# An attention and token-mixing block on one core: weight conversions queued in program order with the channel mixer's activations, and weight loads in larger groups

## The chip, the cores and the metric

The kernel runs on one core of a Trainium2 chip. A core has a matrix engine (TensorE, PE in the profile), a vector engine (VectorE, DVE), an engine for activations (ScalarE, ACT), a general engine (GpSimd, POOL) and SyncE (SP), whose queue issues the DMA transfers here. Each engine works through its own queue in order. Matrix products land in PSUM banks, from which DVE and ACT take them to SBUF. The metric is the device time of one execution in microseconds (us); lower is better.

## What is computed

The reference, cut to what matters (batch 8, 8 heads, 576 rows, head width 64, 128 features; model width 512, hidden width 2048):

```python
def phi(x):
    proj = np.einsum('bhsd,df->bhsf', x, w_phi)
    proj = proj - np.max(np.abs(proj), axis=-1, keepdims=True)
    return np.concatenate([np.exp(proj), np.exp(-proj)], axis=-1)
q_p, k_p = (phi(q), phi(k))
kv = np.einsum('bhsf,bhsd->bhfd', k_p, v)
num = np.einsum('bhsf,bhfd->bhsd', q_p, kv)
den = np.einsum('bhsf,bhf->bhs', q_p, np.sum(k_p, axis=2))[..., None] + 1e-06
x = (num / den)                      # then heads side by side: [8, 576, 512]
u = x + (x.transpose(0, 2, 1) @ U @ V).transpose(0, 2, 1)
out = u + np.maximum(u @ w_ch1, 0.0) @ w_ch2
```

U, V, w_ch1 and w_ch2 come as float64. [...]

## The kernel before

**Stages.** A `Pair` is the attention of two heads of one batch entry; there are 32 pairs. `Tokens` is the U and V product of one batch entry, which starts when its four pairs are done. `Mixer` g is the channel mixer (u @ w_ch1, relu, @ w_ch2) of the 512 rows that batch entry g gives; a ninth mixer takes the remaining 64 rows of all eight. The work of Mixer g is put between the steps of the attention of batch entry g + 1.

**The mixer.** The hidden width goes in 16 tiles of 128. For tile f, `hidden(f)` makes 12 products of 512 columns into one PSUM bank `ph` (L565); ACT takes the relu of it as `h_hi` (L570), DVE the remainder as `h_lo` (L571); `add(f)` makes 12 products into four banks `o` (L582). Each float32 operand is split into a high and a low part, hence the pairs of tiles `uT_hi`/`uT_lo`, `h_hi`/`h_lo`, `w1`/`w2` with two parts. There is one bank `ph` for all mixers but the last, so `hidden(f + 1)` starts only when `h_lo` of tile f has been made. The order in which PE meets these is: ph of tile f, what is left of o of tile f - 1 with attention work between, o of tile f with `h_hi`, ph of tile f + 1, o of tile f with `h_lo`.

**The weights.** The two weight matrices have 16 tiles each, so there are 32 blocks; block `w1_f` is needed by `hidden(f)` and block `w2_f` by `add(f)`, and all mixers use the converted blocks. `load_weights` (L201, L204) issues the loads of one pair of blocks (`words`) on the SP queue; the table `LOADS` says up to which tile they are issued at each of the first pairs. `convert` makes a float32 block from the words: three activations on ACT (L137, L138, L140), two operations on DVE (L141, L142) and one 64-bit addition on GpSimd (L146). `split_w` then splits it: a copy (L223; on ACT for w1, on DVE for w2) and a subtraction on DVE (L224). So a block costs ACT three or four instructions, DVE three or four, GpSimd one. Their work tiles `w_ab` take four buffers, which they share with the split `xs` of the tokens (L507, L508).

**What sets the order.** The program text says when a block is converted: `Pace.step`, called once in each attention step, converts blocks at an even rate between step 24 and step 63, and `mix` converts a block at the latest when the first mixer needs it. The text's order does not bind the engines' queues, though. A scheduler takes the instructions with their dependencies and orders each engine's queue by its own estimate of when each can start. It may put a conversion ahead of an activation that the text has earlier. `tc.issue_after(ins)` takes that freedom away for a block of code: every instruction in it that goes to the engine of `ins` stands behind `ins` in that queue. It adds no wait on a semaphore.

**Names in the rows.** `pp`, `pst`, `vp` are the tokens' products, `pt` the transposes of u, `kv_ps`, `pq`, `pk`, `xp`, `T` those of the attention; `qp`, `kp` are the features, `mk` a maximum, `den` the denominator. In an instruction order, `w2_3_ab` is the work tile of block w2_3, `h_lo0_6` is `h_lo` of Mixer 0 and tile 6; a number behind the name is that of the buffer.

Of the kernel before, what the change touches and what calls it, by code (L numbers as in the profile page):

```python
# [16 lines left out]
AF = mybir.ActivationFunctionType  # L17
# [8 lines left out]
def tile_kernel(  # L26
# [12 lines left out]
    nc = tc.nc  # L39
# [30 lines left out]
    def ps(name, tag="at"):  # L70
        return psum.tile([P, 512], F32, tag=tag, bufs=BANKS[tag], name=name)

    def f32(ap):
        return ap.bitcast(F32)
# [55 lines left out]
    def convert(st, name):  # L130

        n = st.shape[1]
        halves = st.rearrange("p n w -> p (n w)").bitcast(U16).rearrange("p (n h) -> p n h", h=4)
        ab = scratch(f"{name}_ab", I32)
        a, b_ = ab[:, 0, 0:n], ab[:, 1, 0:n]
        bh = b_.bitcast(U16).rearrange("p (n h) -> p n h", h=2)
        nc.scalar.activation(out=bh[:, :, 0], in_=halves[:, :, 1], func=AF.Copy, scale=2.0 ** -13)  # L137
        nc.scalar.activation(  # L138
            out=bh.bitcast(F16)[:, :, 1], in_=f32(st[:, :, 1]), func=AF.Copy, scale=2.0 ** -60)
        nc.scalar.activation(out=f32(a), in_=f32(st[:, :, 1]), func=AF.Abs, scale=2.0 ** -48)  # L140
        nc.vector.tensor_scalar_max(out=f32(a), in0=f32(a), scalar1=2.0 ** -63)  # L141
        nc.vector.tensor_scalar(  # L142
            out=a, in0=a, scalar1=3, scalar2=None, op0=ALU.logical_shift_left)

        a64, b64 = a.bitcast(U64), b_.bitcast(U64)
        nc.gpsimd.int64_add(a64, a64, b64)  # L146
        return f32(a)
# [41 lines left out]
    LAST = NFC - 1  # L189

    def place(f, dt, shape, name):

        if f == LAST:
            both = home.tile([P, 2, *shape], dt, tag="w_last", name=name)
            return both[:, 0], both[:, 1]
        return [home.tile([P, *shape], dt, tag=f"w{n}_{f}", name=f"{name}_{n}") for n in (1, 2)]
# [9 lines left out]
    def convert_block(i):  # L206
        f, n = divmod(i, 2)
        r = convert(words[f][n], f"w{n + 1}_{f}")
        if f < LAST:
            w = home.tile([P, 2, C], F32R, tag=f"w{n + 1}_{f}", name=f"w{n + 1}_{f}")  # L210
            split_w((nc.scalar.copy, nc.vector.tensor_copy)[n], r, w)
        elif n == 0:
            found[f] = r
            return
        else:
            w1_w, w = place(f, F32R, (2, C), f"w_{f}")
            split_w(nc.scalar.copy, found[f], w1_w)
            split_w(nc.vector.tensor_copy, r, w)
            w1_t[f] = w1_w
        (w1_t, w2_t)[n][f] = w  # L220

    def split_w(copy, r, w):
        copy(out=w[:, 0, :], in_=r)  # L223
        nc.vector.tensor_sub(w[:, 1, :], r, f32(w[:, 0, :]))  # L224

    def w1_part(f, part, c):
        return w1_t[f][:, part, c * P:(c + 1) * P]
# [314 lines left out]
    class Mixer:  # L542
# [17 lines left out]
        def hidden(self, f):  # L560
            ph = ps(f"ph{self.g}_{f}", "at" if self.g >= B - 1 and f % 2 == 0 else "ph")
            n = 0
            for c in range(NCC):
                for l, r in ((0, self.uT_hi), (0, self.uT_lo), (1, self.uT_hi)):
                    nc.tensor.matmul(  # L565
                        ph, w1_part(f, l, c), r[:, c, :], start=(n == 0), stop=(n == 3 * NCC - 1))
                    n += 1
            h_hi = moe.tile([P, 512], F32R, tag="h_hi", bufs=2, name=f"h_hi{self.g}_{f}")
            h_lo = moe.tile([P, 512], F32R, tag="h_lo", bufs=2, name=f"h_lo{self.g}_{f}")
            nc.scalar.activation(out=h_hi, in_=ph, func=AF.Relu)  # L570
            nc.vector.scalar_tensor_tensor(  # L571
                out=h_lo, in0=ph, scalar=0.0, in1=f32(h_hi), op0=ALU.max, op1=ALU.subtract)
            self.h[f] = (h_hi, h_lo)

        def add(self, f):
            if self.o is None:
                self.o = [ps(f"o{self.g}_{t}", "o") for t in range(4)]
            h_hi, h_lo = self.h.pop(f)
            for t in range(4):
                cs = slice(t * P, (t + 1) * P)  # L580
                for n, (l, r) in enumerate(((h_hi, 0), (h_hi, 1), (h_lo, 0))):
                    nc.tensor.matmul(  # L582
                        self.o[t], l[:, cs], w2_t[f][:, r, :],
                        start=(f == 0 and n == 0), stop=(f == NFC - 1 and n == 2))
            if f == NFC - 3 and self.g < B:
                self.res = []
                for t in range(0, 4, 2):
                    st = scratch(f"st{self.g}_{t}")
                    nc.sync.dma_start(out=st, in_=u_dram[self.g][:, t:t + 2, :])
                    self.res += [st[:, 0, :], st[:, 1, :]]  # L590
            if f == NFC - 1:
                self.finish()
# [28 lines left out]
    loaded, converted = [0], [0]  # L621

    def weights(upto):

        while loaded[0] <= min(upto, LAST):
            load_weights(loaded[0])
            loaded[0] += 1

    def blocks(upto):
        while converted[0] < min(upto, 2 * NFC):  # L630
            convert_block(converted[0])
            converted[0] += 1

    todo = []
# [1 line left out]
    def mix(n=1):  # L636
        for _ in range(n):
            if todo:
                fn, f = todo.pop(0)
                if fn.__self__.g == 0:  # L640
                    blocks(2 * f + (2 if f == LAST or fn.__name__ == "add" else 1))
                fn(f)
# [3 lines left out]
    class Pace:  # L646
# [5 lines left out]
        def step(self):  # L652

            steps[0] += 1
            blocks((steps[0] - CONVERT[0]) * 2 * NFC // (CONVERT[1] - CONVERT[0]))
            if pieces:
                pieces.pop(0)()
                if not pieces:
                    self.chunks, self.steps = 32 - HELD, BATCH - steps[0]
                else:  # L660
                    keep_busy(1, True)
                return
            n = (self.at + 1) * self.chunks // self.steps - self.at * self.chunks // self.steps
            self.at += 1
            mix(n)
            if not self.chunks:

                keep_busy(1, True)
# [10 lines left out]
            if here:  # L679
                tc.keep_in_program_order(ins)  # L680

    LOADS = (-1, 1, 3, 6, 9, 12, LAST)
    CONVERT = (24, 63)
    BATCH = 67
    pieces = []
# [62 lines left out]
    if True:  # L748
# [17 lines left out]
        for n, (b, j) in enumerate(pairs):  # L766

            far = Pair(*pairs[n + 2]) if n + 2 < len(pairs) else None
            if n < len(LOADS):

                with tc.issue_after(far.loaded.ins):
                    weights(LOADS[n])
            if far is not None:
# [78 lines left out]
```

## Time and profile before

| | us |
|---|---|
| median of 3 runs | 1281.81 |
| the runs | 1281.37, 1281.81, 1289.95 |
| the profiled execution | 1279.61 |
| its span in the trace, from first to last instruction | 1277.8 |

The profiled execution is 1.8 us longer than its span and 2.2 us under the median.

The profile's rows are read so. A stretch of the span is given with the busy time of each engine in it and, in brackets, its instructions. `PEclk` is the share of TensorE's full clock that was granted. An instruction in order of time has its start, its duration, its engine and line, what it writes and reads, and in square brackets for how long the engine sat idle before it and what ended that. A wait is given as engine, instruction, line, then what it waited for, then total us, times, longest.

### The profile page before, as it was taken

The numbers are of one execution on the slowest core, as the hardware profiler recorded it, in microseconds if no ns is written. First come the engines' busy times: TensorE is split into PE (matmuls) and PEld (weight loads), VectorE is DVE, ScalarE is ACT, GpSimd is POOL, SyncE is SP. The second block draws the span as 40 slices with busy tenths as digits, with TensorE's granted clock in tenths as the row PEclk, the third lists the DMA queues.
The fourth block names the chain that finished last, engine by engine and source line by source line (L and its number), as shares of the span: only waits on it lengthen the run. The fifth ranks groups of instructions, "written<-read, shape, count | busy, mean of one in ns | idle before, by whom it ended". The sixth has DMA issues, their size and how long they took to land.

```text
span 1277.8 us, 17927 instructions
## 1 busy us (share of the span) xinstructions
PE 1240.0 (97%) x6939; PEld 1062.0 (83%) x6941; DVE 649.2 (51%) x1441; ACT 540.3 (42%) x1151; POOL 201.2 (16%) x154
## 2 busy tenths in 40 slices
PE   8988979999999999999999999999999999999997
PEld 7766868878888888888888888888888888788886
DVE  5879585565456545455556545545545542211211
ACT  6887484444443444344444435344434431111110
POOL 3444242101110111111110111011111110000000
PEclk9998989999999999999999999999999999999999
DMA  5582131220122111211112012211122002100001
GB/s 137 172 275 72 62 125 28 61 85 25 38 60 80 29 29 45 82 62 29 45 45 89 13 28 68 90 28 29 45 78 66 17 1 87 66 1 1 33 1 33
DMA packets 90100, 75.38 MB, mean 59 GB/s; under 512 B 51488, under 2 KB 76448, under 8 KB 89888
## 3 DMA queue, kind: packets, MB, share of 16 engines
q1 hardware_dynamic: 90016, 74.24, 19.1%
q8 instruction: 55, 0.90, 0.3%
q14 instruction: 29, 0.24, 0.1%
HBM read 55.35 MB, written 18.87 MB: 58 GB/s over the span
## 4 chain that ended last, share of the span: by engine, by line
PE 88%; DVE 6%; ACT 3%; issue 1%; DMA 1%; SPq 0%; POOL 0%; DVEq 0%; POOLq 0%; ACTq 0%
PE ph L565 31%; PE o L582 30%; PE kv_ps L411 7%; PE xp L450 7%; PE T L291 2%; PE pk L371 2%; PE pp L521 1%; PE pq L394 1%; PE kv_ps L404 1%; PE xpt L437 1%; DVE w L224 1%; PE pq L395 1%; PE pt L553 1%; DVE w_ab L141 1%; DVE w_ab L142 1%
## 5 line engine op out<-in xcount | busy, mean ns | idle before, releaser
L565 PE MATMUL ph<-uT_hi,w 128*128 128x512 f32 x1152 | 388.8, 396 | 7.5 <-DVE h_lo L571 6.6
L582 PE MATMUL o<-w,h_hi 128*128 128x512 f32 x1152 | 326.1, 395 | 1.0 <-ACT h_hi L570 1.0
L565 PEld LDWEIGHTS ph<-uT_hi,w 128*128 128x128 f32 x1152 | 217.3, 189 | 51.7 <-DVE h_lo L571 7.8
L582 PEld LDWEIGHTS o<-w,h_hi 128*128 128x128 f32 x1152 | 211.5, 188 | 43.0 <-ACT h_hi L570 2.4
L571 DVE SCALAR_TENSOR_TENSOR h_lo<-ph,h_hi 128x512 fp32r<-128x512 f32 x144 | 99.4, 690 | 265.9 <-ACT h_hi L570 265.2
L565 PE MATMUL ph<-uT_lo,w 128*128 128x512 f32 x576 | 228.4, 396 | 0.9 <-DVE uT_lo L232 0.9
L570 ACT ACTIVATE h_hi<-ph 128x512 fp32r<-128x512 f32 x144 | 86.1, 598 | 309.2 <-PE ph L565 299.6
L582 PE MATMUL o<-w,h_lo 128*128 128x512 f32 x576 | 191.4, 398 | 0.0
L335 POOL PARTITION_ALL_REDUCE qp<-qp x64 | 126.2, 1973 | 364.1 <-ACT qp L334 355.1
L450 PEld LDWEIGHTS xp<-kv,qp 128*128 128x128 f32 x1024 | 122.9, 192 | 7.5 <-ACT qp L337 2.6
L565 PEld LDWEIGHTS ph<-uT_lo,w 128*128 128x128 f32 x576 | 109.1, 189 | 24.0 <-DVE uT_lo L232 3.0
L411 PEld LDWEIGHTS kv_ps<-vb,kp 128*128 128x128 f32 x1024 | 124.1, 195 | 4.3 <-issue 2.3
L450 PE MATMUL xp<-kv,qp 128*128 128x65 f32 x1024 | 123.8, 273 | 2.7 <-ACT qp L337 1.5
L582 PEld LDWEIGHTS o<-w,h_lo 128*128 128x128 f32 x576 | 106.4, 188 | 21.3 <-issue 1.0
L411 PE MATMUL kv_ps<-vb,kp 128*128 128x65 f32 x1024 | 123.7, 275 | 0.1
L274 DVE TENSOR_TENSOR T<-T,T 64x512 fp32r<-64x512 f32 x96 | 66.2, 689 | 82.1 <-ACT T L273 80.9
L273 ACT CAST T<-T 64x512 fp32r<-64x512 f32 x96 | 55.9, 582 | 101.5 <-PE pq L395 72.4
L335 POOL PARTITION_ALL_REDUCE qp_t<-qp_t x32 | 25.2, 788 | 379.8 <-ACT qp_t L334 379.8
L325 ACT ACTIVATE kp<-kp 128x512 f32<-128x512 f32 x64 | 40.3, 630 | 63.1 <-DVE kp L322 49.5
L374 ACT COPY kp<-pk 128x256 f32<-128x256 f32 x96 | 35.6, 372 | 70.3 <-PE pk L371 69.9
L375 DVE TENSOR_TENSOR kp<-pk,kp 128x256 f32<-128x256 f32 x96 | 40.2, 419 | 34.1 <-ACT kp L374 33.7
L146 POOL INT64_ADD w_ab<-w_ab x32 | 43.9, 1371 | 66.9 <-DVE w_ab L142 48.5
(126 smaller groups left out, 1386.0 us busy)
## 6 DMA issues: line engine op xcount, KB each, us to landing
words<-in_moe_w_ch_dram SPq DMA_DIRECT2D x32, 512.0 KB, 7.7
raw<-in_k_dram SPq DMA_DIRECT2D x32, 256.0 KB, 2.8
raw<-in_q_dram SPq DMA_DIRECT2D x32, 256.0 KB, 3.1
vb<-in_v_dram SPq DMA_DIRECT2D x64, 128.0 KB, 2.6
u_dram<-x SPq DMA_DIRECT2D x32, 256.0 KB, 2.5
st<-u_dram SPq DMA_DIRECT2D x16, 512.0 KB, 4.3
out_dram<-st SPq DMA_DIRECT2D x32, 256.0 KB, 2.5
t_r<-in_k_dram SPq DMA_DIRECT2D x32, 32.0 KB, 2.2
```

What stands on the lines that cost most here:

```text
L146: nc.gpsimd.int64_add(a64, a64, b64)
L273: nc.scalar.copy(out=dst[0:D], in_=src)
L274: nc.vector.tensor_sub(dst[D:2 * D], src, f32(dst[0:D]))
L325: nc.scalar.activation(out=kp[:, :, 0:F], in_=kp[:, :, F:2 * F], func=AF.Exp)
L335: nc.gpsimd.partition_all_reduce(qp[:, 0, :], qp[:, 1, :], P, ReduceOp.absmax)
L375: nc.vector.tensor_tensor(out=k_w[:, ts_, :], in0=pk[:, :, 0, :], in1=kp[:, ts_, 0:F], op=ALU.add)
L411: nc.tensor.matmul(self.kv_v[:, f, g, :], kp[:, t, f * F:(f + 1) * F], self.vb[:, g, t, :], start=False, stop=(t == NT - 1), skip_group_ch ...
L450: nc.tensor.matmul(xv[:, c, :], qp[:, f, c * P:(c + 1) * P], self.kv[:, f, c // 2, :], start=(f == 0), stop=(f == 1))
L565: nc.tensor.matmul(ph, w1_part(f, l, c), r[:, c, :], start=(n == 0), stop=(n == 3 * NCC - 1))
L570: nc.scalar.activation(out=h_hi, in_=ph, func=AF.Relu)
L571: nc.vector.scalar_tensor_tensor(out=h_lo, in0=ph, scalar=0.0, in1=f32(h_hi), op0=ALU.max, op1=ALU.subtract)
L582: nc.tensor.matmul(self.o[t], l[:, cs], w2_t[f][:, r, :], start=(f == 0 and n == 0), stop=(f == NFC - 1 and n == 2))
```

## The change

Two things are changed. First, each mixer activation pair (`h_hi` on ACT, `h_lo` on DVE) of Mixer 0 is put on a list, and when a block is converted, all of its instructions on ACT and DVE are queued behind the last pair that the text has made so far. Second, `LOADS` groups the weight tiles differently: two, three, four, four and three tiles in five groups in place of two, two, three, three, three and three in six.

```diff
-            nc.scalar.activation(out=h_hi, in_=ph, func=AF.Relu)
-            nc.vector.scalar_tensor_tensor(
+            on_act = nc.scalar.activation(out=h_hi, in_=ph, func=AF.Relu)
+            on_dve = nc.vector.scalar_tensor_tensor(
                 out=h_lo, in0=ph, scalar=0.0, in1=f32(h_hi), op0=ALU.max, op1=ALU.subtract)
             self.h[f] = (h_hi, h_lo)
+            if self.g == 0:
+                made.append((on_act, on_dve))
...
+    made = []
+
     def blocks(upto):
         while converted[0] < min(upto, 2 * NFC):
-            convert_block(converted[0])
+            with ExitStack() as order:
+
+                for ins in made[-1:]:
+                    for i in ins:
+                        order.enter_context(tc.issue_after(i.ins))
+                convert_block(converted[0])
             converted[0] += 1
...
-    LOADS = (-1, 1, 3, 6, 9, 12, LAST)
+    LOADS = (-1, 1, 4, 8, 12, LAST)
```

No instruction is added or removed; the engines' queues are ordered differently. All differences lie in the part of the program up to the first tiles of Mixer 1; behind that the queues are alike. Three places show it.

The first is ACT's queue while the tokens of the first batch entry are worked on, behind the conversion of w1_3. Before:

```order
L137 ACTIVATE w2_3_ab_1194<-words3_2_676 128x512
L138 ACTIVATE w2_3_ab_1194<-words3_2_676 128x512
L140 ACTIVATE w2_3_ab_1194<-words3_2_676 128x512
L524 CAST pst0_593<-pp0_1_990 128x256
L137 ACTIVATE w1_4_ab_1228<-words4_1_834 128x512
L138 ACTIVATE w1_4_ab_1228<-words4_1_834 128x512
L140 ACTIVATE w1_4_ab_1228<-words4_1_834 128x512
L337 ACTIVATE qp1_0_0_984<-qp1_0_0_984 128x512
L137 ACTIVATE w2_4_ab_1301<-words4_2_835 128x512
L138 ACTIVATE w2_4_ab_1301<-words4_2_835 128x512
```

After, from the same place on:

```order
L524 CAST pst0_593<-pp0_1_998 128x256
L337 ACTIVATE qp1_0_0_992<-qp1_0_0_992 128x512
L338 ACTIVATE qp1_0_0_992<-qp1_0_0_992 128x512
L223 CAST w1_3_1141<-w1_3_ab_1134 128x512
L300 COPY T1_1_1_1039<-T1_1_1_1034 128x512
L334 COPY qp1_0_1_1094<-pq1_1_0_1092 128x512
L231 CAST uT_hi0_1059<-pt0_0_1061 128x4x128
L231 CAST uT_hi0_1059<-pt0_1_1068 128x4x128
L231 CAST uT_hi0_1059<-pt0_2_1110 128x4x128
L231 CAST uT_hi0_1059<-pt0_3_1117 128x4x128
```

The conversions from w2_3 on have moved from here to behind `h_hi` of tile 0. On DVE, 56 conversion instructions stood ahead of `h_lo` of tile 0, and 30 do now.

The second is DVE's queue ahead of `h_lo` of tile 7 of Mixer 0; the fences show the last rows of that tile. Before:

```order
L142 TENSOR_SCALAR w1_12_ab_1990<-w1_12_ab_1990 128x512
L417 COPY kv1_2_1789<-kv_ps1_2_1752 128x260
L141 TENSOR_SCALAR w2_12_ab_2044<-w2_12_ab_2044 128x512
L142 TENSOR_SCALAR w2_12_ab_2044<-w2_12_ab_2044 128x512
L141 TENSOR_SCALAR w1_13_ab_2085<-w1_13_ab_2085 128x512
L142 TENSOR_SCALAR w1_13_ab_2085<-w1_13_ab_2085 128x512
L141 TENSOR_SCALAR w2_13_ab_2170<-w2_13_ab_2170 128x512
L142 TENSOR_SCALAR w2_13_ab_2170<-w2_13_ab_2170 128x512
L336 TENSOR_TENSOR qp1_2_1_1765<-qp1_2_1_1765 128x512
L224 TENSOR_TENSOR w1_12_1997<-w1_12_ab_1990,w1_12_1997 128x512
L320 TENSOR_REDUCE mk1_3_t_1843<-pkt1_3_1840 128x1
L571 SCALAR_TENSOR_TENSOR h_lo0_7_1815<-ph0_7_1801,h_hi0_7_1814 128x512
```

After, all that stands between `h_lo` of tile 6 and that of tile 7:

```order
L141 TENSOR_SCALAR w1_9_ab_1741<-w1_9_ab_1741 128x512
L142 TENSOR_SCALAR w1_9_ab_1741<-w1_9_ab_1741 128x512
L141 TENSOR_SCALAR w2_9_ab_1782<-w2_9_ab_1782 128x512
L142 TENSOR_SCALAR w2_9_ab_1782<-w2_9_ab_1782 128x512
L223 CAST w2_9_1789<-w2_9_ab_1782 128x512
L141 TENSOR_SCALAR w1_10_ab_1802<-w1_10_ab_1802 128x512
L224 TENSOR_TENSOR w2_9_1789<-w2_9_ab_1782,w2_9_1789 128x512
L417 COPY kv1_2_1800<-kv_ps1_2_1763 128x260
L224 TENSOR_TENSOR w1_9_1748<-w1_9_ab_1741,w1_9_1748 128x512
L142 TENSOR_SCALAR w1_10_ab_1802<-w1_10_ab_1802 128x512
L224 TENSOR_TENSOR w1_10_1809<-w1_10_ab_1802,w1_10_1809 128x512
L571 SCALAR_TENSOR_TENSOR h_lo0_7_1826<-ph0_7_1812,h_hi0_7_1825 128x512
```

There were 20 conversion instructions between these two activations, running up to block w2_13, and there are 10 now, up to w1_10. Counted in the same way from each `h_lo` to the next, from tile 0 to tile 11, DVE's queue held 8, 1, 0, 0, 5, 9, 20, 11, 3, 0, 0, 0 conversion instructions and holds 6, 5, 9, 5, 10, 4, 10, 4, 9, 8, 7, 6 now. ACT's held 7, 1, 0, 0, 6, 10, 21, 10, 1, 0, 0, 0 and holds 6, 4, 10, 4, 11, 3, 11, 3, 10, 8, 7, 6.

The third is the queue of SP at the fourth pair's loads (`words` 4 to 6 before, 5 to 8 now). Before:

```order
L248 DMA raw1_1_1_829<-in_q_dram 128x2x256
L201 DMA words4_1_834<-in_moe_w_ch1_dram 128x4x256
L204 DMA words4_2_835<-in_moe_w_ch2_dram 128x1024
L201 DMA words5_1_838<-in_moe_w_ch1_dram 128x4x256
L204 DMA words5_2_839<-in_moe_w_ch2_dram 128x1024
L201 DMA words6_1_842<-in_moe_w_ch1_dram 128x4x256
L204 DMA words6_2_843<-in_moe_w_ch2_dram 128x1024
L265 DMA vb1_97<-in_v_dram 128x4x64 x2
```

After:

```order
L248 DMA raw1_1_1_833<-in_q_dram 128x2x256
L201 DMA words5_1_838<-in_moe_w_ch1_dram 128x4x256
L204 DMA words5_2_839<-in_moe_w_ch2_dram 128x1024
L201 DMA words6_1_842<-in_moe_w_ch1_dram 128x4x256
L204 DMA words6_2_843<-in_moe_w_ch2_dram 128x1024
L201 DMA words7_1_846<-in_moe_w_ch1_dram 128x4x256
L204 DMA words7_2_847<-in_moe_w_ch2_dram 128x1024
L201 DMA words8_1_850<-in_moe_w_ch1_dram 128x4x256
L204 DMA words8_2_851<-in_moe_w_ch2_dram 128x1024
L265 DMA vb1_97<-in_v_dram 128x4x64 x2
```

The loads of tiles 4 and up have moved one group earlier or joined a larger one, and the values of the pair (`vb`) stand behind one or two more weight tiles.

## The prediction

> **What bounds the kernel now.** I read the page first, then the stretches of the first 290 us, then PE's own waits in them, then single engines in order of time.
>
> ```profile
> span 1277.8 us, 17927 instructions
> PE 1240.0 (97%) x6939; PEld 1062.0 (83%) x6941; DVE 649.2 (51%) x1441; ACT 540.3 (42%) x1151; POOL 201.2 (16%) x154
> ...
> PE   8988979999999999999999999999999999999997
> ...
> DVE  5879585565456545455556545545545542211211
> ...
> PEclk9998989999999999999999999999999999999999
> ```
>
> PE is the bound: it is idle for 37.8 us of the span. The digits show where time can be won: only in the first slices of 32 us, where DVE is busiest and the clock digit twice falls to 8. Cut by stage, with the conversions' share (tile `w_ab`) below:
>
> ```profile
> core 0: us, PE busy (x) PEld busy (x) DVE busy (x) ACT busy (x) POOL busy (x), PEclk, DMA share, GB/s
> 76.00:115.00 39.00, 28.44 (x148) 21.52 (x148) 35.72 (x70) 37.01 (x71) 19.98 (x15) 0.87 0.44 138
> 115.00:155.00 40.00, 39.72 (x214) 33.38 (x215) 23.36 (x50) 19.36 (x42) 9.77 (x8) 1.00 0.31 100
> 155.00:200.00 45.00, 37.04 (x171) 30.25 (x170) 37.95 (x61) 32.77 (x59) 22.32 (x16) 0.85 0.28 91
> 200.00:255.00 55.00, 55.00 (x322) 47.65 (x321) 28.12 (x66) 25.30 (x55) 10.03 (x6) 1.00 0.18 52
> 255.00:290.00 35.00, 33.02 (x197) 28.44 (x196) 21.88 (x48) 13.90 (x30) 2.68 (x2) 1.00 0.27 86
> ```
>
> ```profile
> 76.00:115.00 39.00, 22.12 (x36) 26.68 (x43) 14.67 (x11) 0.87 0.44 138
> 115.00:155.00 40.00, 10.52 (x15) 5.05 (x8) 4.07 (x3) 1.00 0.31 100
> 155.00:200.00 45.00, 29.93 (x42) 26.16 (x42) 17.78 (x13) 0.85 0.28 91
> 200.00:255.00 55.00, 2.73 (x6) 2.56 (x4) 1.52 (x1) 1.00 0.18 52
> ```
>
> The second fence gives DVE, ACT and POOL only. Conversions come in two bursts, 76 to 115 and 155 to 200, and only there is DVE busy for 92% and 84% of the time, PE idle (10.56 and 7.96 us) and the clock down. PE's waits name the place:
>
> ```profile
> PE ph L565 <- DVE h_lo L571: 6.6, 3, 4.1
> PE kv_ps L404 <- DVE pst L525: 2.5, 1, 2.5
> PE pq L397 <- DVE kv L417: 2.1, 1, 2.1
> PE T L291 <- ACT qp L334: 1.9, 1, 1.9
> PE pt L553 <- DVE xt L538: 1.4, 1, 1.4
> ```
>
> ```profile
> 115.05 0.50 PE L565 MATMUL ph<-uT_hi,w 128*128 128x512 f32 x1 [2.32 <-DVE h_lo L571]
> 187.80 0.80 PE L565 MATMUL ph<-uT_hi,w 128*128 128x512 f32 x1 [4.08 <-DVE h_lo L571]
> ```
>
> PE waits for short DVE results that stand behind conversions in an ordered queue. In front of the first of these two:
>
> ```profile
> 110.51 0.41 DVE L141 TENSOR_SCALAR w_ab<-w_ab 128x512 f32<-128x512 f32 x1
> 110.96 1.41 DVE L142 TENSOR_SCALAR w_ab<-w_ab 128x512 int32<-128x512 int32 x1
> ...
> 114.32 0.68 DVE L571 SCALAR_TENSOR_TENSOR h_lo<-ph,h_hi 128x512 fp32r<-128x512 f32 x1
> ```
>
> ```profile
> 110.79 1.30 POOL L146 INT64_ADD w_ab<-w_ab  x1 [1.74 <-ACT qp_t L334]
> ```
>
> The same kind of conversion takes 0.41 us alone and 1.41 us while a 64-bit addition runs on POOL. Over the four stages a conversion instruction holds DVE for (22.12 + 10.52 + 29.93 + 2.73) / 99 = 0.66 us.
>
> **The ceiling.** Between 76 and 200 us PE loses 10.56 + 0.28 + 7.96 = 18.8 us idle, and 0.13 x 39 + 0.15 x 45 = 5.1 + 6.75 = 11.8 us of clock: 30.6 us, slightly too much, since idle time at half clock counts in both. Behind 200 us nothing of it is left to win; the 1.98 us idle in 255 to 290 belong to the second tokens' stage. The Trainium skill, "TensorE: Matmul & The Clock Gate", Part 1 (What's actually happening), says that the clock is halved after at least one idle window of about 3.4 us. Here 0.87 stands in a stretch whose longest wait is 2.3 us, so the trace does not agree; by the rule the small waits below would cost no clock, and my sum would come out 3.4 us lower.
>
> **Part A, tokens, 76 to 115 us.** The order takes 56 - 30 = 26 conversion instructions off DVE's queue ahead of the first `h_lo`: 26 x 0.66 = 17.2 us of DVE in 28 us. ACT shows the same:
>
> ```profile
> 83.78 0.80 ACT L137 ACTIVATE w_ab<-words 128x512 uint16<-128x512 uint16 x1
> ...
> 85.04 0.68 ACT L140 ACTIVATE w_ab<-words 128x512 f32<-128x512 f32 x1
> 85.59 0.39 ACT L524 CAST pst<-pp 128x256 fp32r<-128x256 f32 x1
> ```
>
> `pst` stands behind block w2_3, which takes 85.59 - 83.78 = 1.81 us, and would start at 83.78. Ceiling here: 10.56 + 5.1 = 15.6 us. What stays: the 1.9 us wait of T for qp, earlier and untouched. What comes newly late is the chain of the tokens itself: about 0.9 us for `pst` where pq waited 2.1, about 1 us for the additions to x (1.4 before), about 1.2 us for the last `uT_lo` in place of the waits for kp, xt and `h_lo`. Sum 5.0, so A gains 10.6. Bounds: 13 (only the 1.9 and 0.7 for `pst` stay), and 6 (one more wait of 1.2 and one spell at half clock, 3.4).
>
> **Part B, tiles 0 to 11.** What leaves 155 to 200 goes to the tiles of Mixer 0, evenly. The measure is one tile's time on PE:
>
> ```profile
> 122.35 0.68 DVE L571 SCALAR_TENSOR_TENSOR h_lo<-ph,h_hi 128x512 fp32r<-128x512 f32 x1
> ...
> 153.41 0.69 DVE L571 SCALAR_TENSOR_TENSOR h_lo<-ph,h_hi 128x512 fp32r<-128x512 f32 x1
> ...
> 203.84 0.69 DVE L571 SCALAR_TENSOR_TENSOR h_lo<-ph,h_hi 128x512 fp32r<-128x512 f32 x1 [1.90 <-ACT h_hi L570]
> ...
> 245.23 0.69 DVE L571 SCALAR_TENSOR_TENSOR h_lo<-ph,h_hi 128x512 fp32r<-128x512 f32 x1 [1.99 <-ACT h_hi L570]
> ```
>
> Tiles 1 to 5 take 31.06 / 4 = 7.8 us each, tiles 9 to 14 41.39 / 5 = 8.3, both with PE full. DVE's other work is (23.36 - 10.52) / 5 = 2.6 us a tile in the one stage and (28.12 - 2.73) / 7 = 3.6 in the other. A late `h_lo` does no harm as long as PE has the previous tile's o products, a row of which is
>
> ```profile
> 133.46 2.83 PE o L582 x12
> ```
>
> so about 2.7 us of lateness is covered. Before, tiles 6 and 7 hold 20 and 11 conversions: 31 x 0.66 + 2 x 2.6 - 2 x 7.8 - 2.7 = 7.4 us lost, near the 7.96 measured; the count is fit for use. Now the fullest tiles hold 10: tile 4, which also splits the second tokens, 6.6 + 3.6 + some 1.2 for `xs` = 11.4, over 7.8 + 2.7 by 0.9; tile 6 6.6 + 2.6 = 9.2, none; tiles 8 and 9 together 17 x 0.66 + 7.2 = 18.4 against 16.6 + 2.7, none. I charge 1 us. In all, 83 x 0.66 + 12 x 3.1 = 92 us of DVE stand against 12 x 8.0 = 96 of PE: DVE is 96% full, so this is no comfortable fit. ACT: 11 conversions at 0.60 (1.81 / 3) in tiles 4 and 6 are 6.6 us ahead of the next `h_hi`, plus features; I charge 2 us for chains ACT, DVE, POOL, DVE that arrive late. And I keep one spell of half clock of 6.8 us, cost 3.4, since waits of about 2 us brought it before. Stays: 6.4. Ceiling 7.96 + 6.75 = 14.7, so B gains 8.3. Bounds: 13.7 (only the 1 us stays) and 0 (below).
>
> The Trainium skill, "GPSIMD Engine Reference", Key points, says that GpSimd shares its SBUF interfaces with VectorE and contends with two-port modes and with two SBUF inputs. The 1.41 us row agrees; the rule speaks against the change, since the number of additions stays the same and each still stretches a DVE instruction wherever it is put.
>
> **Loads.** Nothing, either way. A tile costs SP two issues:
>
> ```profile
> 64.24 0.46 SPq L201 DMA_DIRECT2D words<-in_moe_w_ch_dram  x1
> 64.76 0.49 SPq L204 DMA_DIRECT2D words<-in_moe_w_ch_dram  x1
> ```
>
> ```profile
> words<-in_moe_w_ch_dram SPq DMA_DIRECT2D x32, 512.0 KB, 7.7
> vb<-in_v_dram SPq DMA_DIRECT2D x64, 128.0 KB, 2.6
> ```
>
> That is about 1 us a tile, 2 us later at most for `vb` behind it. Tiles 5 to 8 are issued from about 64 us; at 138 GB/s or more their 4 MB take under 31 us, while w1_7 is first touched behind `h_hi` of tile 4, about three tiles of 7.8 after 122.35, less A's 10.6: past 130 us. The values serve the pair after next, so a whole pair's work covers them. If a cover were gone, 7.7 us of landing would show once per group.
>
> **Sum.** A 10.6 + B 8.3 = 18.9 us. From the profiled execution's 1279.6 (span 1277.8 plus 1.8) that gives 1260.7; the runs' median stands 2.2 us higher, so I predict 1281.8 - 18.9 = 1263.
>
> **Rivals.** *Nearly all comes back:* A 12.6 (3.0 stay), B 13.7, 26.3 in sum, 1255.5. For it: DVE's count covers every tile but one. Against: it leaves nothing for chains over three ordered queues.
>
> *Half comes back:* the four tiles with 9 or 10 conversions (2, 4, 6, 8) each cost 2 us and two spells of half clock 6.8 together, so B gains nothing, and A has one spell of 3.4 and gains 7.2: 1274.6. For it: DVE 96% full, and tile 4, which held 5 conversions without loss, now holds 10 beside the token split.
>
> *Slower, latency instead of throughput:* in a tile with three blocks, `h_lo` waits for 3 x 1.81 = 5.4 us of ACT, two DVE operations 1.3, an addition 1.3 behind an all-reduce 2.0 on POOL, copy and subtraction 1.3, itself 0.7: 12.0 us. If PE's next ph (2.7) starts only then, the tile takes 14.7 in place of 8.0; five such tiles (2, 4, 6, 8, 9) lose 33.5, B becomes 14.7 - 33.5 = -18.8 and the time 1281.8 - 10.6 + 18.8 = 1290. The all-reduce is this row of the page:
>
> ```profile
> L335 POOL PARTITION_ALL_REDUCE qp<-qp x64 | 126.2, 1973 | 364.1 <-ACT qp L334 355.1
> ```
>
> The kernel ends slower once those five tiles pass 8.0 + (14.7 + 10.6) / 5 = 13 us each. Against: PE's order puts o products and attention between, and `h_hi`/`h_lo` have two buffers.
>
> *The loads arrive late:* 7.7 us in each of two groups, which leaves 3.5 of the gain: 1278.
>
> **How the numbers follow.** Forecast 0.58, nearly all 0.14, half 0.20, slower 0.06, loads 0.02. About 1% (12.8 us, under 1269) is what a measurement of this kernel tells from no change. Faster: the forecast's own range, 1256 to 1271 by its bounds' middle parts, lies under 1269 to nine tenths, 0.54, plus 0.14: 0.68. Within 1%: 0.04 + 0.20 + 0.02 = 0.26. Slower by over 1%: the latency case is worth +0.7% at its price and more if the clock stays down; I give its whole 0.06 to that side. The range takes in the forecast, most of the nearly-all and of the half case: 1254 to 1276.
>
> **What would show it.** In the stretch from 76 us to `h_hi` of tile 0, no conversion behind w1_3 and the first ph of tile 1 near 104 us instead of 115.05 (A right). `h_lo` rows 7 to 9 us apart from tile 0 to 11, with no wait over 2.5 us on ph (B right); a wait at tile 4 or 5, or a clock under 0.95 in the stretch that follows, shows the half case. Gaps of 13 us between `h_lo` rows show the latency case; a PE or ACT wait on `words` shows the loads. From the second tokens on, all should be the old trace shifted; a difference there would make the sum wrong.

## The result and the profile after

| | median, us | runs | profiled execution (span) |
|---|---|---|---|
| before | 1281.59 | 4, the profiled one among them, 1279.62 to 1289.95 | 1279.6 (1277.8) |
| changed | 1265.58 | 4, 1265.06 to 1265.94 | 1265.06 (1263.3) |

The changed kernel is 1.3% faster: ratio 0.9872, 95% interval 0.9847 to 0.9897, 16.0 us by the medians. The two spans differ by 14.5 us; the other 1.5 us come from how the two profiled executions stand to their medians, 2.0 and 0.5 us below. The prediction was 1263.

The head of the page of the changed kernel, the same rows as those shown of before:

```profile
span 1263.3 us, 17913 instructions
PE 1234.8 (98%) x6941; PEld 1059.5 (84%) x6941; DVE 648.0 (51%) x1441; ACT 540.0 (43%) x1151; POOL 202.2 (16%) x154
...
PE   8989999999999999999999999999999999999997
...
DVE  5877787745455545545455545654545542212111
...
PEclk9999998999999999999999999999999999999999
```

PE's instructions are the same. Its idle time fell from 37.8 to 28.5 us, and its busy time by 5.2 us, because less of the work ran at half clock. The clock digit falls to 8 once (the slice from 190 us) where it did so twice. DVE's two peaks have become one plateau. The first five stages of the changed kernel, in the columns used before:

```profile
76.00:115.00 39.00, 34.90 (x209) 29.19 (x210) 29.93 (x59) 29.18 (x59) 15.77 (x11) 1.00 0.71 227
115.00:155.00 40.00, 37.30 (x205) 30.95 (x204) 31.68 (x60) 28.86 (x58) 16.47 (x12) 1.00 0.22 72
155.00:200.00 45.00, 41.80 (x220) 34.83 (x218) 36.86 (x68) 34.12 (x64) 21.02 (x15) 0.92 0.09 24
200.00:255.00 55.00, 52.64 (x285) 44.37 (x284) 38.62 (x85) 27.71 (x59) 9.90 (x7) 0.97 0.25 79
255.00:290.00 35.00, 35.00 (x211) 30.85 (x210) 15.68 (x39) 14.00 (x30) 4.62 (x3) 1.00 0.10 26
```

The prediction counted a stage's loss as PE's idle time plus what the clock withheld. In 76 to 115 us that is now 4.10 us with a full clock, where it was 15.6. In 115 to 200 us it is 2.70 + 3.20 idle and 0.08 x 45 = 3.6 of clock, 9.5 where it was 15.0. Behind 200 us it is 2.36 + 0.03 x 55 = 4.0, where 1.98 stood. That makes 11.5 + 5.5 - 2.0 = 15.0 us, against 14.5 in the spans, so the count holds. Who PE waits for from 76 to 290 us:

```profile
PE kv_ps L404 <- issue: 2.8, 1, 2.8
PE o L584 <- ACT h_hi L570: 2.0, 2, 1.0
PE T L291 <- ACT qp L334: 1.9, 1, 1.9
PE ph L565 <- ACT uT_hi L231: 1.4, 2, 0.7
PE xpt L437 <- DVE kp L375: 1.1, 1, 1.1
PE vp L537 <- DVE pst L525: 1.0, 1, 1.0
PE pq L397 <- ACT qp_t L334: 0.7, 1, 0.7
...
PE ph L565 <- DVE h_lo L571: 0.4, 1, 0.4
```

The 6.6 us of `ph` waiting for `h_lo` that headed the list before are 0.4. A new row heads it: one wait of 2.8 us before `kv_ps`, with no releaser named ("issue"). What frees it is found in the order of time. These are rows of DVE, and of PE where marked, between 186 and 192 us:

```profile
186.34 1.78 DVE L336 TENSOR_TENSOR qp<-qp 128x512 f32<-128x512 f32 x1
188.04 0.41 DVE L141 TENSOR_SCALAR w_ab<-w_ab 128x512 f32<-128x512 f32 x1
...
188.82 0.28 DVE L274 TENSOR_TENSOR tail_T<-tT,tail_T 64x128 fp32r<-64x128 f32 x1
...
190.32 1.26 DVE L224 TENSOR_TENSOR w<-w_ab,w 128x512 fp32r<-128x512 f32 x1
...
191.61 0.29 DVE L274 TENSOR_TENSOR tail_T<-tT,tail_T 64x128 fp32r<-64x128 f32 x1
...
192.00 0.68 PE L404 MATMUL kv_ps<-vt,kp_t 128*128 128x130 f32 x4 [2.79 <-issue]
```

`kv_ps` takes one of the three PSUM banks of the attention. By this reading the one it waits for holds `tT`, the transposed tails of pair 2_0, the first pair that is split into high and low parts. The second subtraction on `tail_T` ends at 191.61 + 0.29 = 191.90, and 0.10 us later PE starts. That subtraction stood behind conversion rows in DVE's queue (L141, L224). Two of the rows ahead of it are also longer than usual: L336 takes 1.78 us and L224 1.26 us while POOL runs 64-bit additions (from 186.03 and from 189.77 us); rows of the same two lines and sizes with nothing on POOL beside them take 0.67 to 0.69 us. Up to here this is a reading; experiments e5 and e7 test it.

### The profile page after: what moved, and what is told of

The parts are those of the page before. It is cut to its first block, busy times and chain, and to the rows that moved or that the text cites. A ratio compares the mean times of both kernels' runs of the same rounds, so it can differ in the third digit from the quotient of the medians.

```text
span 1263.3 us, 17913 instructions
## 1 busy us (share of the span) xinstructions
PE 1234.8 (98%) x6941; PEld 1059.5 (84%) x6941; DVE 648.0 (51%) x1441; ACT 540.0 (43%) x1151; POOL 202.2 (16%) x154
## 4 chain that ended last, share of the span: by engine, by line
PE 87%; ACT 5%; DVE 5%; issue 2%; DMA 1%; POOL 1%; SPq 0%; DVEq 0%; POOLq 0%; ACTq 0%
PE ph L565 30%; PE o L584 29%; PE kv_ps L411 7%; PE xp L450 7%; PE T L291 2%; PE pk L371 2%; PE pp L521 1%; PE xpt L437 1%; PE pt L553 1%; PE pq L394 1%; PE kv_ps L404 1%; ACT w_ab L138 1%; ACT w_ab L137 1%; PE pq L395 1%; ACT w_ab L140 1%
```

## The experiments

Each ratio is to the kernel before, run beside it on the same chip, with its 95% interval.

**e1, e2: the order alone, the loads alone.** e1 is the changed kernel with the old `LOADS`, e2 the kernel before with the new one.

```
-    LOADS = (-1, 1, 4, 8, 12, LAST)
+    LOADS = (-1, 1, 3, 6, 9, 12, LAST)
```

> The new order of the conversions with the old grouping of the loads. Theory (the order alone carries the change, the loads are worth nothing): 1265.6 us, the time of the changed kernel, within 2 us. Rival (the grouping of the loads has a part in the gain or takes some of it back): more than 3 us away from 1265.6 to either side.

> The old order with the new grouping of the loads. Theory: 1281.6 us, the time of the kernel before, within 2 us. Rival (the loads have a part): under 1279; a rival the other way (loads late): over 1284.

e1 took 1265.80 us (0.9877, 0.9843 to 0.9910), e2 1280.42 (1.0005, 0.9977 to 1.0032). Both theories hold: the order of the conversions carries the change, and the grouping of the loads is worth nothing that these runs can tell from zero.

**e3, e4: part A alone, part B alone.** In e3 the blocks wait for tile 0's activations only; in e4 nothing is held before block 17, w2_8.

```
-                for ins in made[-1:]:
+                for ins in made[:1]:
```

```
-                for ins in made[-1:]:
+                for ins in made[-1:] if converted[0] >= 17 else ():
```

> The conversions wait only for the activations of tile 0; behind that they run ahead freely, as before (part A alone). The prediction's size of A: 10.6 us, so 1271.0. Theory now (A was sized too small, since the lead at tile 0 is 15.0 us): 1266 to 1268. Rival (the gain belongs to both parts about equally): 1273 or more. The second burst, if it still costs what it did, shows as PE idle time and half clock in the stretch behind tile 5.

> Only the conversions from block w2_8 on are held behind the activations, so the burst ahead of tile 0 is as before and the second one is spread (part B alone). The prediction's size of B: 8.3 us, so 1273.3. Theory now (B gives little by itself, since the lead of 15.0 us at tile 0 and the gain of 14.5 us at the end of the trace are nearly the same): 1279 to 1282. If the parts add up, e3's gain and e4's gain make 16.0.

e3 took 1266.00 us (0.9879, 0.9850 to 0.9908), e4 1274.77 (0.9948, 0.9921 to 0.9975). So A by itself gives 15.2 us, as e3's theory had it, and B by itself 6.4; together they give 16.0, not 21.6. The theory that B by itself gives nothing falls, and so does the idea that the parts add up: once tile 0 is held, holding the later blocks adds 0.4 us by the medians, less than these runs can tell from nothing. The stages of e3:

```profile
76.00:115.00 39.00, 33.15 (x184) 27.42 (x185) 31.79 (x63) 31.81 (x63) 17.73 (x12) 0.93 0.70 222
115.00:155.00 40.00, 39.29 (x210) 33.02 (x209) 34.24 (x62) 25.98 (x53) 16.92 (x12) 0.99 0.22 73
155.00:200.00 45.00, 40.24 (x211) 34.20 (x209) 38.64 (x71) 35.88 (x67) 23.07 (x15) 0.92 0.09 21
200.00:255.00 55.00, 53.17 (x308) 45.69 (x308) 36.38 (x73) 25.95 (x55) 8.00 (x5) 1.00 0.29 91
```

By the same count e3 loses 5.85 + 0.07 x 39 = 8.6 us in the first row, 0.71 + 0.40 + 4.76 + 3.60 = 9.5 in the next two, and 1.8 in the last. The changed kernel loses 4.1, 9.5 and 4.0 there. In 115 to 200 us the two lose the same, with and without the later blocks held. Only the place differs. In e3 PE waits behind a smaller burst, 4.49 us for one chain of DVE, whose rows come after PE's:

```profile
178.65 0.66 PE L450 MATMUL xp<-kv,qp 128*128 128x65 f32 x2 [4.49 <-DVE kp_t L322]
```

```profile
175.54 1.50 DVE L141 TENSOR_SCALAR w_ab<-w_ab 128x512 f32<-128x512 f32 x1
...
177.62 0.68 DVE L336 TENSOR_TENSOR qp<-qp 128x512 f32<-128x512 f32 x1
178.22 0.28 DVE L322 TENSOR_TENSOR kp_t<-pkt,mk_t 128x128 f32<-128x128 f32 x1
```

What the holding of later blocks does gain beside A is 8.6 - 4.1 = 4.5 us ahead of 115 us, where in e3 the released blocks stand right behind the activations of tiles 0 and 1, and it gives 2.2 us back behind 200 us. Of the 4.5 us 2.7, and of the 2.2 us 1.65, are clock in one traced execution each, so only the rest is firm.

**e5: the stacks of the split pair first.** The two blocks that the text converts behind pair 2_0's transposes are queued behind its `tail_T` copies and subtractions, which are now the last entry of the list, in place of the last activation pair.

```
-            nc.scalar.copy(out=dst[0:D], in_=src)
-            nc.vector.tensor_sub(dst[D:2 * D], src, f32(dst[0:D]))
+            i = nc.scalar.copy(out=dst[0:D], in_=src)
+            return i, nc.vector.tensor_sub(dst[D:2 * D], src, f32(dst[0:D]))
...
-                        self.stack(tv, self.tail_T[:, :, r_])
+                        stacked = self.stack(tv, self.tail_T[:, :, r_])
+                        if self.nm == "2_0":
+                            made.append(stacked)
```

> As the changed kernel, but the two blocks of weights that are converted behind the transposes of pair 2_0 (w2_12 and w1_13) also wait for that pair's tail_T stacks. Theory (the 2.79 us wait of PE before kv_ps at 192 us comes from the tail_T subtraction that stands behind conversions on DVE and keeps an attention bank, and the half clock behind it, 3.2 us, comes from that wait): the wait goes, the clock in 190 to 200 us stays at 1.00, and the time is about 1265.6 - 6.0 = 1259.6 us. Rival (DVE is full there, whatever stands first is paid by what stands next): the wait moves to ph of tile 10 or 11 and the time stays within 2 us of 1265.6.

1263.34 us (0.9874, 0.9835 to 0.9914), with runs from 1260.89 to 1272.25. It was run again as a control of e10:

> Experiment e5 once more beside e10 on the same chip, as its control. Theory: 1261 to 1263 us in most runs and about 1272 us in some, as in e5. Rival (e5's long runs were an accident of that chip): all runs 1261 to 1264 us.

1263.17 us (0.9875, 0.9843 to 0.9907), runs from 1261.74 to 1272.55, as its theory had it. In e11's trace the subtractions stand ahead, `kv_ps` starts without a wait, and the clock is full; the stage loses 0.96 us where the changed kernel loses 6.8. Its rows of DVE, of PE, and of the stage:

```profile
185.73 0.28 DVE L274 TENSOR_TENSOR tail_T<-tT,tail_T 64x128 fp32r<-64x128 f32 x1
...
186.64 0.29 DVE L274 TENSOR_TENSOR tail_T<-tT,tail_T 64x128 fp32r<-64x128 f32 x1
```

```profile
189.15 0.61 PE L406 MATMUL kv_ps<-vt,kp_t 128*128 128x130 f32 x4
```

```profile
155.00:200.00 45.00, 44.04 (x245) 36.94 (x245) 37.04 (x68) 33.85 (x64) 21.29 (x15) 1.00 0.11 27
```

So the cause of the wait is shown, and with it the half clock left this place. But only part of the expected 6.0 us reached the end: the median of the 11 runs of e5 and e11 is 1263.3, against 1265.6 for the changed kernel, and their mean, 1265.5, is hardly better than the 1265.8 of the changed kernel's eight runs (e12 below). One reason stands in the same trace, and the rival has it in part: other waits come in place of the one that went, above all for the subtractions that make `T`, which now stand behind conversions.

```profile
192.03 1.10 PE L399 MATMUL pq<-T,w_two 128*128 128x512 f32 x2 [0.54 <-DVE T L274]
```

With one of 0.82 us for `T` before `pk` (at 202.11 us) and two smaller ones, 0.17 for `kv` and 0.29 for `h_hi`, PE waits 1.8 us there that it did not wait before, against the 2.79 that went; e5's own trace has the same four waits. The other reason is that three of the 11 runs took 1271 to 1273 us. The next run asks why.

**e10: products of zeros in an early wait.** e5's profiled execution was one of the long ones. One window of its trace, then the same of e11's:

```profile
56.20:73.30 17.10, 17.10 (x74) 15.60 (x75) 6.86 (x19) 6.32 (x14) 4.72 (x4) 0.50 0.27 81
```

```profile
56.20:73.30 17.10, 16.45 (x122) 14.15 (x120) 12.94 (x38) 10.94 (x24) 6.54 (x6) 1.00 0.59 195
```

In the 6.2 us ahead of it PE is busy for 4.62 and 4.63 us, at full clock in both, and the longest wait is all but the same, each trace's own row:

```profile
54.78 0.44 PE L452 MATMUL xp<-kv,qp 128*128 128x65 f32 x2 [1.47 <-ACT qp L339]
```

```profile
54.56 0.44 PE L452 MATMUL xp<-kv,qp 128*128 128x65 f32 x2 [1.46 <-ACT qp L339]
```

One execution then ran 17.1 us at half clock, which is 8.55 us lost, and the other none. e10 fills this wait.

```
-                keep_busy(1, True)
+                keep_busy(7 if steps[0] == 18 else 1, True)
```

> Experiment e5 with six more idle products of zeros on PE in the wait of 1.5 us before xp at 53 to 54 us, far ahead of the change. Theory (the long runs of e5, 1271 and 1272 us against 1261 to 1263, come from a spell of half clock that begins in this wait and lasted 17.1 us in its profiled run): no run over 1266 us, median 1262. Rival (the long runs have another cause): runs of 1270 us and more remain. The six products take 1.3 us at most, inside the wait.

1265.26 us (0.9873, 0.9849 to 0.9897), six runs from 1261.77 to 1267.54. In its trace the wait is 0.20 us, so it is filled. No run of 1270 us is left, which speaks for the theory, but weakly: at three in 11, six runs without one would come with a chance of (8/11)^6 = 0.15. The median is a miss: it did not fall to 1262. In e10's trace the clock is 0.87 in 76 to 115 us, where e11's is 1.00, so half clock came in another place.

**e6: the final additions later.**

```
...
-                    nc.vector.tensor_add(st, st, self.o[t])
+                    with ExitStack() as order:
+                        if g == 0 and t > 1:
+                            order.enter_context(tc.issue_after(turned[1, 1].ins))
+                        nc.vector.tensor_add(st, st, self.o[t])
...
```

(`turned[g, t]` is the subtraction that makes `uT_lo` of mixer g and token tile t.)

> As the changed kernel, but the last two of Mixer 0's four final additions (st) stand behind the second uT_lo of Mixer 1 on DVE, not in front of it. Theory (the loss of 5.7 us in 240 to 256 us comes from these additions ahead of uT_lo): PE's waits there fall by 1 to 2 us and the half clock goes, so 1262.5 to 1264.5 us. Rival (the stage is limited by the banks that the additions free, for pt of the third and fourth token tiles): 1265.6 us, or up to 2 us slower.

1269.01 us (0.9895, 0.9866 to 0.9925): slower than the changed kernel by 3.4. The theory falls: with the last two additions moved back, the loss behind 240 us does not go. (By the count used above that loss is 4.0 us, not 5.7.) In its trace `xpt` waits 1.8 us for `kp_t`, where in the changed kernel it waits 1.1 for `kp`. PE's idle time from 200 to 255 us is the same, 2.34 us against 2.36; what grew is the time at half clock, 0.93 against 0.97 there and 0.91 against 1.00 from 255 to 290 us.

**e7: without the additions on POOL.**

```
-        nc.gpsimd.int64_add(a64, a64, b64)
+        if name[0] != "w":
+            nc.gpsimd.int64_add(a64, a64, b64)
```

> As the changed kernel without the 64-bit additions of the weights' conversions on POOL (the weights' values are then not those of the reference; U's and V's conversions keep theirs). Theory of the prediction (DVE is 96% full in the 12 tiles, much of it because an addition stretches a DVE instruction from 0.41 to 1.41 us): most of the 10.6 us that PE still loses between 115 and 200 us goes, so 1256 to 1259 us. Rival (what is left is one place in the order, the stacks of the first split pair behind conversions, with DVE's share elsewhere of no account): the wait before kv_ps stays and the time is 1263 to 1266 us.

1252.06 us (0.9764, 0.9740 to 0.9788), 13.5 us under the changed kernel and below what either theory gave. (The 10.6 us of the expectation are 9.5 by the count used above.) The group of one conversion line on DVE, minimum, median and maximum in ns, first of the changed kernel, then of e7:

```profile
L141 DVE TENSOR_SCALAR w_ab<-w_ab x32: 410/428/1481, 43.2 to 232.3; 128x512 f32<-128x512 f32 x32
```

```profile
L141 DVE TENSOR_SCALAR w_ab<-w_ab x32: 405/426/448, 44.1 to 222.3; 128x512 f32<-128x512 f32 x32
```

The long ones of this line are gone. Conversions (tile `w_ab`) hold DVE for 50.49 / 99 = 0.51 us each in e7, against 62.30 / 99 = 0.63. PE then has no idle time and a full clock from 115 to 200 us:

```profile
115.00:155.00 40.00, 40.00 (x218) 34.03 (x217) 29.45 (x69) 34.16 (x67) 5.42 (x4) 1.00 0.20 61
155.00:200.00 45.00, 45.00 (x254) 38.27 (x254) 32.19 (x73) 33.35 (x66) 7.27 (x4) 1.00 0.11 28
```

The wait before `kv_ps` is gone too, so the additions had a part in it beside the order. e7 takes away the stretching and also one step of 1.3 us from each block's chain, and the scheduler orders the rest anew; how the 13.5 us divide between these was not tried.

**e8, e9: a more even spread**, with and without e5's edit.

```
-    CONVERT = (24, 63)
+    CONVERT = (22, 63)
```

> Experiment e5 (the stacks of the first split pair ahead of two blocks) with the conversions begun two steps earlier (CONVERT from 22 in place of 24), which leaves at most 5 conversion products per tile on DVE where the changed kernel has 6. Theory (what is left between the tiles are single fullest places: the stacks, and tile 4 with 2.0 us of PE waiting for h_hi): e5's undisturbed 1262 us less 2 us, 1260 us; against the kernel before about 0.983. Rival (an even spread is worth nothing once the stacks stand first): 1262 to 1264 us.

> The changed kernel with the conversions begun two steps earlier, without e5's edit. Theory (tile 4's 2.0 us go, the wait before kv_ps and its half clock stay): 1263.6 us, 2 us under the changed kernel. Rival (the even spread also takes the wait before kv_ps away, since only the amount of DVE work per tile counts): 1260 us. Rival (nothing changes): 1265.6 us.

e8 took 1265.45 us (0.9885, 0.9858 to 0.9912), e9 1268.89 (0.9899, 0.9870 to 0.9928). Both miss on the slower side. The wait of `o` for `h_hi` did not go; it is one wait of 2.1 us instead of two of 1.0. e9's five runs spread from 1262.49 to 1271.81. Its profiled one, the 1262.49, has the wait before `kv_ps` and no half clock behind it:

```profile
194.15 0.68 PE L404 MATMUL kv_ps<-vt,kp_t 128*128 128x130 f32 x4 [2.27 <-issue]
```

```profile
192.00:200.00 8.00, 5.86 (x42) 5.26 (x43) 7.16 (x12) 7.03 (x13) 2.54 (x2) 1.00 0.11 23
```

**e12: the changed kernel again.**

> The changed kernel once more, to see how far its own runs spread beside the 11 of e5 and e11 (1260.9 to 1272.6, median 1263.3). Theory (each longer wait of PE brings a spell of half clock in some runs and not in others, and the changed kernel has one such wait more than e5): most runs 1264 to 1269, median 1265 to 1267, so 2 us over e5's. Rival (e5's edit is worth nothing): median under 1264.

1265.49 us (0.9880, 0.9864 to 0.9896), four runs from 1265.08 to 1268.11, as the theory had it. The median over all eight runs of the changed kernel stays 1265.6; e5's version is 2.3 us better by its median and 0.3 by its mean, so whether it beats the changed kernel is open.

## Why the prediction was right, and where it was not

**A, right.** The sum left 5.0 us in 76 to 115; 4.1 are left. The waits are those it named: T for `qp` 1.9, as it was; `vp` for `pst` 1.0, against 0.9; and 0.7 for a `uT` that is last, against 1.2. The chain of additions to x costs nothing where 1 us was set aside. The first `ph` of tile 1 starts at 103.20 us, where "near 104" was said, behind nothing but PE's own work:

```profile
100.96 2.40 PE L584 MATMUL o<-w,h_hi 128*128 128x512 f32 x8
103.20 0.39 PE L565 MATMUL ph<-uT_hi,w 128*128 128x512 f32 x1
```

The stage gained 15.6 - 4.1 = 11.5 against 10.6. Which wait for an activation earns it is another matter than the prediction's two parts suggest. Held for tile 0 only (e3), the blocks give 15.6 - 8.6 = 7.0 us here and already 15.0 - 9.5 = 5.5 in 115 to 200 us, all that the changed kernel gains there; the rest of A comes from holding the later blocks, and by the medians of whole runs it is worth 0.4 us.

**B, the term that was mis-sized.** "Stays: 6.4" should have been 9.5. Its own parts came out well: 3 us for tile 4 and late chains, measured 2.0 for `o` behind `h_hi` (at tiles 5 and 6, none at tile 4) and 0.7 for `pq`; 3.4 us for one spell of half clock, measured 3.6. That the spell fits is luck, since it came behind the wait that the working did not have. What was missing is the wait of 2.79 us before `kv_ps`, plus 0.4 on `ph`. The working looked for late activations and counted DVE by tiles; it did not ask which other short results on DVE free a bank. e5 shows that wait's cause.

"DVE is 96% full" was wrong too. The work was sized well: 92 us were said, and DVE is busy for 89.1 us between the first and the last of these 13 rows. The time of a tile was not: 8.0 us were said, and the 12 tiles took (212.95 - 99.32) / 12 = 9.5.

```profile
99.32 0.69 DVE L571 SCALAR_TENSOR_TENSOR h_lo<-ph,h_hi 128x512 fp32r<-128x512 f32 x1 [0.78 <-ACT h_hi L570]
...
212.95 0.69 DVE L571 SCALAR_TENSOR_TENSOR h_lo<-ph,h_hi 128x512 fp32r<-128x512 f32 x1 [0.36 <-ACT h_hi L570]
```

So DVE is 89.1 / 113.6 = 78% full. Of the 9.5 us, 0.8 are idle time and half clock, (6.0 + 3.4) / 12. The other 8.7 are more than 8.0 for one reason at least: the stretch from tile 1 to tile 5 was cut where PE still owed products, 40 into `o` lie in it where four tiles have 48. The sign "`h_lo` rows 7 to 9 us apart" failed: five of the 12 gaps are 10.8 to 12.8 us, without a wait on `ph` over 0.4 us. The one from 113.75 to 124.72 us holds no wait of PE at all, so it is PE's own work, the attention between the tiles, and no sign of the latency case.

**The second tokens, wrong.** "Behind 200 us nothing of it is left to win" and "all should be the old trace shifted" did not hold. The stage loses 4.0 us where it lost 1.98. Its idle time is nearly the same, 2.36 us; what is new are 1.65 us of clock. e6 moved the last two of the four additions and did not remove it; what brings it was not settled.

**The loads, right:** e2's interval holds 1, and e1 without the new grouping takes the changed kernel's time.

**The sum.** Predicted 18.9; by the same count 11.5 + 5.5 - 2.0 = 15.0; by the medians 16.0. The direction and the main mechanism stand. The 3.9 us between 18.9 and 15.0 are 2.8 too much in B and 2.0 in the second tokens, less 0.9 that A gave over its size; the medians show 1 us more gain than the count because the two profiled executions stand differently to their medians. That the total came out near is in part luck: the sum took A and B as independent, and e3 and e4 show that they are not, 15.2 and 6.4 us alone and 16.0 together. The half case's signs did show, a wait at tile 5 (1.03 us before `o` at 144.50 us) and a clock under 0.95 in 155 to 200 us (0.92), but B did not lose what that case charged, and the clock fell behind `kv_ps`, not behind a full tile.

**The additions on POOL.** The Trainium skill, "GPSIMD Engine Reference", Key points, has GpSimd contending with VectorE for the SBUF interfaces. The prediction took from it that the additions would go on stretching DVE wherever they are put. The traces agree: e7 shows it for L141, and L224, with both inputs in SBUF, takes 0.67 to 1.79 us in the changed kernel; a row of 1.77 us, at 181.47 us, runs beside an addition (minimum, median, maximum in ns):

```profile
L224 DVE TENSOR_TENSOR w<-w_ab,w x32: 671/684/1789, 47.1 to 235.8; 128x512 fp32r<-128x512 f32 x32
```

e7 gives 13.5 us for the stretching and the shorter chains together. `h_lo`, with one of its two inputs in PSUM, is not stretched: in e11 one lies wholly inside an addition and takes its usual 0.69 us.

```profile
192.54 1.54 POOL L146 INT64_ADD w_ab<-w_ab  x1 [2.00 <-DVE w_ab L142]
192.97 0.69 DVE L573 SCALAR_TENSOR_TENSOR h_lo<-ph,h_hi 128x512 fp32r<-128x512 f32 x1
```

The additions are not alone in this. e7 has none of them on the weights, and its other conversion line on DVE still has long rows; the longest, 1.38 us, starts at 103.32 us, inside an all-reduce on POOL that starts at 103.09 and takes 2.29.

```profile
L142 DVE TENSOR_SCALAR w_ab<-w_ab x32: 399/427/1384, 44.6 to 222.7; 128x512 int32<-128x512 int32 x32
```

## What to carry to other kernels

Spreading a burst of fill work over the stages that have room pays where the burst stood ahead of a short result that PE waits for, and almost all of the pay came from the first such place; behind it, the loss moved to the next short result in the same ordered queue, and in e5 it moved on once more. So list every short DVE or ACT step that frees a PSUM bank, not the activations alone, before sizing what stays. Where a wait is taken away and the time falls by less than the wait, look for the waits that came in its place (here 1.8 of 2.8 us), and compare the clock in several traced executions. Parts of a change that are each worth something alone need not add up, so run each alone and both together.

## What the runs showed of the hardware

The clock answers to the same wait differently from one execution to the next. A wait of 1.46 to 1.47 us was followed by 17.1 us at half clock in one execution and by none in another; a wait of 2.79 us by 6.8 us, in the windows of the changed kernel below. In e12, the same kernel, the same wait (2.77 us) is followed by one spell of 3.4 us (196.0 to 199.4 us, clock 0.51), and the wait of 2.27 us in e9 by none. That a spell is brought by the wait ahead of it is read from their order in time; e10, which fills one wait, is the only test of it here.

```profile
185.00:192.60 7.60, 4.73 (x23) 3.74 (x23) 7.38 (x14) 4.50 (x11) 2.86 (x3) 1.00 0.16 53
192.60:199.40 6.80, 6.80 (x29) 5.77 (x28) 4.62 (x9) 4.63 (x9) 2.98 (x3) 0.50 0.12 27
```

The spells last 3.4, 6.8 and 17.1 us, one, two and five times 3.4. The Trainium skill, "TensorE: Matmul & The Clock Gate", Part 1 (What's actually happening), has a free-running window of 3413 ns, and with that the lengths agree, and the chance in them too. Its condition, a whole idle window, does not: none of these waits lasts 3.4 us. A spell costs half its length, 1.7, 3.4 and 8.55 us here, as much as some terms of the sum; the runs of e5 lie up to 11.4 us apart, with mean clocks from 0.987 to 0.997.

A 64-bit addition on POOL can stretch a DVE instruction between SBUF tiles from 0.41 to as much as 1.48 us (L141 of the changed kernel), and an all-reduce on POOL does so too, to 1.38 us (L142 of e7). `h_lo`, which reads PSUM, stays at 0.69 us inside an addition (e11).
